# Pair transposes with scores on two row tiles, tables by symmetry and row shifts, and later weights: one change to a linear-attention and Fourier-mix kernel

## The chip, the cores and the metric

One core of one Trainium2 chip. The metric is device time in microseconds of one execution. On one core a run counts as slow when it lies over 1.5% above the fastest of the same kernel.

A ratio below is the mean time of one kernel's fast runs over that of the kernel before's fast runs in the same rounds, with a 95% interval. It is therefore not quite the ratio of the medians that stand beside it.

## The reference

Two parts, one behind the other. The first is an attention with a state that decays per channel, over 4 batches, 8 heads, 768 positions, head width 48:

```python
for t in range(S):
    cur = einsum('bhd,bhe->bhde', u * k_t, v_t)
    y_t = einsum('bhd,bhde->bhe', r_t, state + cur)
    state = w_t[..., None] * state + einsum('bhd,bhe->bhde', k_t, v_t)
```

The second takes y as 768 x 384 per batch:

```python
mixed = real(fft(fft(x, axis=1), axis=2))
u  = x + mixed
un = (u - mean(u)) / sqrt(var(u) + 1e-6)          # over the 384 channels
out = u + relu(un @ w_ch1) @ w_ch2                # 384 -> 1536 -> 384
```

## The kernel before

The attention goes in chunks of 128 positions, 6 a batch, 24 in all. I call them chunk 1 to 24; batch 0 is chunks 1 to 6. For each chunk SyncE loads w, k, r and v (0.2 MB each, in rows of 48 floats), ScalarE takes the logarithm of w, TensorE sums it along the positions, ScalarE takes the exponentials, VectorE and GpSimd scale r and k, TensorE transposes both, and ScalarE copies the transposes to SBUF. The part that the change rewrites, with cuts:

```python
def tr_r(e):                       # r: eight transposes, one for each head
    for h in range(H):
        o0 = 128 * h - 64 * (h % 2)
        ins = e.transpose(psb(trr)[:, 128*h:128*h+128], rflat[:, o0:o0+128], IDB[:, :])
...
op("act", 1000, ... e.activation(rT, psb(trr)[:, :], Copy))      # 1024 columns
...
for hf in range(2):
    def amat(e, hf=hf, ta=ta):     # scores: four matmuls of 256 columns
        for x in range(2):
            q = 2 * hf + x
            ins = e.matmul(ps(ta)[:, 256*x:256*x+256], kT[:, q, :], rT[:, 2*q:2*q+2, :])
```

The Fourier mix is done with matmuls against tables of sines and cosines, which VectorE and ScalarE build at the start. CS and SS serve the sequence axis, DTM and DTP the channel axis. All arguments were computed on VectorE at full width, and DTM had its own argument for each row.

The instructions are put in order by a planner in the kernel itself. It walks through the operations with an assumed duration each and emits every engine's queue in the order of the planned starts. Every queue then runs in that order. For loads it keeps one clock for all queues:

```python
elif o.bytes:
    dma_t = max(dma_t, s + o.dur) + o.bytes / 190.0
    o.end = dma_t + self.DMA_FIX
```

The weights are asked for on GpSimd's queue, because they are converted to bf16 on the way. In the kernel before that was allowed once chunk 3's v had landed.

Of the kernel before, what the change touches and what calls it, by code (L numbers as in the profile page):

```python
# [28 lines left out]
class _Op:  # L29
    __slots__ = ("eng", "fn", "deps", "users", "dur", "key", "tile", "opens", "sem", "inc", "val",  # L30
                 "start", "end", "nd", "idx", "clk", "bytes", "order", "waits", "ready", "last")
# [16 lines left out]
class _Prog:  # L48
# [18 lines left out]
    def op(self, eng, dur, fn, r=(), w=(), key=None, sem=None, nbytes=0):  # L67
# [3 lines left out]
        o.bytes = nbytes  # L71
        for x in r:
            for d in self.wr.get(x, ()):
                o.deps.add(d)
            self.rd.setdefault(x, []).append(o)
            if isinstance(x, _Tile):
                o.tile = (o.tile or []) + [x]
# [18 lines left out]
    def schedule(self):  # L96
# [5 lines left out]
        dma_t = 0.0  # L102
        for o in self.ops:
            for d in o.deps:
                d.users.append(o)
            o.nd = len(o.deps)
            o.ready = 0.0
            if o.nd == 0:
                avail[o.eng].append(o)
        left = len(self.ops)  # L110
        while left:
            best = None
            for e in self.ENGS:
                t = engt[e]
                cand = None
                for o in avail[e]:
                    s = max(t, o.ready)
                    if o.opens:
                        tl = [x for x in o.tile if x.bank is None and x.ops[0] is o][0]
                        if held.get(tl.pool, 0) >= self.caps[tl.pool] or not free_banks:  # L120
                            continue
                        s = max(s, free_banks[0][0])
                    c = (s, o.key, o.idx)
                    if cand is None or c < cand[0]:
                        cand = (c, o)
                if cand and (best is None or cand[0] < best[0]):
                    best = cand
# [4 lines left out]
            if o.opens:  # L132
                tl = [x for x in o.tile if x.bank is None and x.ops[0] is o][0]
                _, tl.bank, prev = heapq.heappop(free_banks)
                held[tl.pool] = held.get(tl.pool, 0) + 1
                o.deps |= set(prev)
            o.start = s
            engt[e] = s + o.dur
            if o.bytes:
                dma_t = max(dma_t, s + o.dur) + o.bytes / 190.0  # L140
# [134 lines left out]
def bass_rwkv6_finch__then__fnet_fourier_mix_kernel(  # L275
# [16 lines left out]
    HF = S // 2 + 1  # L292
    NJ = HID // 128
# [4 lines left out]
    g = _Prog(nc, {"a": 5, "f": 4})  # L298
# [11 lines left out]
    E1 = [sb("e1_%d" % i, [H, D], FP32) for i in range(NB)]  # L310
    E2 = [sb("e2_%d" % i, [H * D + HP], FP32) for i in range(NB)]
    RH = [sb("rh%d" % i, [H, 128], BF16) for i in range(NB)]
    KH = [sb("kh%d" % i, [H, 64], BF16) for i in range(NB)]
    VB = [sb("vb%d" % i, [H, D], BF16) for i in range(4)]
    RTB = [sb("rtb%d" % i, [H, 128], BF16) for i in range(NB)]
# [15 lines left out]
    NMU = [sb("nmu%d" % i, [1], FP32) for i in range(4)]  # L331
# [10 lines left out]
    IDB = sb("idb", [128], BF16)  # L342
# [5 lines left out]
    KI = sb("ki", [HF], FP32)  # L348
    CI = sb("ci", [128], FP32)
    TC = sb("tc", [NC], FP32)  # L350
    TN = sb("tn", [NC], FP32)
    MC = sb("mc", [3], FP32)
    MN = sb("mn", [3], FP32)
    MSH = sb("msh", [3], FP32)
    MB = sb("mb", [3], FP32)
    IS1 = sb("is1", [1], FP32)
    TMPC = sb("tmpc", [4], FP32)
    CP = sb("cp", [1], FP32)
    ALT = sb("alt", [HF], BF16)
# [3 lines left out]
    TF = [sc_u[:, HF * i:HF * i + HF] for i in range(5)] + [sc_h[:, 0:HF]]  # L363
    TG = [sc_h[:, HF * i:HF * i + HF] for i in range(1, 4)]
    TQ = [sc_h[:, HF * 4:HF * 5], sb("tq", [HF], FP32)]
# [7 lines left out]

    def tt(o, a, b, f):
        return lambda e: e.tensor_tensor(out=o, in0=a, in1=b, op=f)  # L375

    def ts(o, a, s1, s2, f0, f1=None):
        if f1 is None:
            return lambda e: e.tensor_scalar(out=o, in0=a, scalar1=s1, scalar2=None, op0=f0)
        return lambda e: e.tensor_scalar(out=o, in0=a, scalar1=s1, scalar2=s2, op0=f0, op1=f1)  # L380

    def stt(o, a, s, b, f0, f1):
        return lambda e: e.scalar_tensor_tensor(out=o, in0=a, scalar=s, in1=b, op0=f0, op1=f1)
# [19 lines left out]
    def small_constants():  # L403
        op("pool", 250, lambda e: e.iota(CI[:, :], [[1, 128]], base=0, channel_multiplier=-1,
                                         allow_small_or_imprecise_dtypes=True), w=["CI"])
        op("pool", 250, lambda e: e.iota(TC[:, :], [[128, NC]], base=0, channel_multiplier=1,
                                         allow_small_or_imprecise_dtypes=True), w=["TC"])
        op("pool", 450, lambda e: e.iota(KI[:, :], [[1, HF]], base=0, channel_multiplier=0,
                                         allow_small_or_imprecise_dtypes=True), w=["KI"])
        op("dve", 210, ts(MSK[:, :], CI[:, :], 0.0, None, ALU.is_gt), r=["CI"], w=["MSK"])  # L410
        op("dve", 210, ts(NLE[:, :], CI[:, :], 0.0, -1.0, ALU.is_ge, ALU.mult), r=["CI"], w=["NLE"])
        op("dve", 270, fill(LB[0][:, :, :], 0.0), w=[("LB", 0)])
        op("dve", 70, fill(ONE[:, :], 1.0), w=["ONE"])
        op("dve", 70, fill(BHPI[:, :], PI / 2), w=["BHPI"])
        op("dve", 490, fill(RH[0][:, :, :], 0.0), w=[("RH", 0)])
        op("dve", 210, ts(IDB[:, :], CI[:, :], 0.0, None, ALU.is_equal), r=["CI"], w=["IDB"])
        op("pool", 580, fill(KH[0][:, :, :], 0.0), w=[("KH", 0)])
        op("dve", 270, fill(LB[1][:, :, :], 0.0), w=[("LB", 1)])
        op("dve", 490, fill(RH[1][:, :, :], 0.0), w=[("RH", 1)])
        op("pool", 580, fill(KH[1][:, :, :], 0.0), w=[("KH", 1)])  # L420
        op("dve", 70, fill(BEPS[:, :], EPS), w=["BEPS"])
        for i in range(2, NB):
            op("dve", 270, fill(LB[i][:, :, :], 0.0), w=[("LB", i)])
            op("dve", 490, fill(RH[i][:, :, :], 0.0), w=[("RH", i)])
            op("pool", 580, fill(KH[i][:, :, :], 0.0), w=[("KH", i)])
        for i in range(2):
            op("pool", 400, fill(XF[i][:, :, 0:64], 0.0), w=[("XFz", i)] + [("XFn", i)])
            op("pool", 400, fill(XF[i][:, :, 446:512], 0.0), w=[("XFz2", i)] + [("XFo", i, c) for c in range(NC)])
            op("pool", 120, fill(X[i][:, :, DM:DM + 4], 0.0), w=[("X", i, c) for c in range(NC)])
# [3 lines left out]
    def tables():  # L433
        sins = []
        op("dve", 100, ts(TN[:, :], TC[:, :], 1.0 / S, None, ALU.mult), r=["TC"], w=["TN"])

        op("dve", 350, ts(TQ[0][:, :], KI[:, :], 0.5, MAGIC, ALU.mult, ALU.add), r=["KI"], w=[("TQ", 0)])
        op("dve", 350, ts(TQ[1][:, :], TQ[0][:, :], MAGIC, -2.0, ALU.subtract, ALU.mult),
           r=[("TQ", 0)], w=[("TQ", 1)])
        op("dve", 550, tt(TQ[0][:, :], KI[:, :], TQ[1][:, :], ALU.add), r=["KI", ("TQ", 1)], w=[("TQ", 0)])  # L440
        op("dve", 550, tt(TQ[1][:, :], TQ[0][:, :], TQ[0][:, :], ALU.mult), r=[("TQ", 0)], w=[("TQ", 1)])
        op("dve", 350, ts(ALT[:, :], TQ[1][:, :], -2.0, 1.0, ALU.mult, ALU.add), r=[("TQ", 1)], w=["ALT"])
        sc = 2.0 * PI / S * (1.0 - 2.0 ** -22)
        for q in range(NC // 2):
            op("dve", 350, ts(TQ[0][:, :], KI[:, :], TN[:, q:q + 1], MAGIC, ALU.mult, ALU.add),
               r=["KI", "TN"], w=[("TQ", 0)])
            op("dve", 350, ts(TQ[1][:, :], TQ[0][:, :], MAGIC, -float(S), ALU.subtract, ALU.mult),
               r=[("TQ", 0)], w=[("TQ", 1)])
            op("dve", 550, stt(TF[q][:, :], KI[:, :], TC[:, q:q + 1], TQ[1][:, :], ALU.mult, ALU.add),
               r=["KI", "TC", ("TQ", 1)], w=[("TF", q)])  # L450
            op("dve", 550, stt(TG[q][:, :], TF[q][:, :], -1.0, TF[q][:, :], ALU.mult, ALU.max),
               r=[("TF", q)], w=[("TG", q)])
            sins.append(act(SS[:, q, :], TF[q][:, :], ACTF.Sin, scale=sc))
            sins.append(act(CS[:, q, :], TG[q][:, :], ACTF.Sin, scale=-sc, bias=BHPI[:, :]))

        p = TC[:, 0:1]
        op("dve", 100, ts(IS1[:, :], p, 62.5, None, ALU.is_gt), r=["TC"], w=["IS1"])
        op("dve", 100, ts(TMPC[:, 0:1], IS1[:, :], -193.0, 129.0, ALU.mult, ALU.add), r=["IS1"], w=["TM0"])
        op("dve", 100, ts(TMPC[:, 1:2], p, 63.0, 193.0, ALU.is_equal, ALU.mult), r=["TC"], w=["TM1"])
        op("dve", 100, tt(TMPC[:, 2:3], TMPC[:, 0:1], TMPC[:, 1:2], ALU.add), r=["TM0", "TM1"], w=["TM2"])  # L460
        op("dve", 100, tt(TMPC[:, 3:4], TMPC[:, 2:3], p, ALU.add), r=["TM2", "TC"], w=["TM3"])
        op("dve", 100, ts(CP[:, :], IS1[:, :], 2.0, -1.0, ALU.mult, ALU.add), r=["IS1"], w=["CP"])
        op("dve", 100, tt(MC[:, 1:2], TMPC[:, 3:4], CP[:, :], ALU.mult), r=["TM3", "CP"], w=["MC1"])
        op("dve", 100, ts(MC[:, 0:1], p, 64.0, None, ALU.add), r=["TC"], w=["MC0"])
        op("dve", 100, ts(MC[:, 2:3], p, -1.0, -1.0, ALU.mult, ALU.add), r=["TC"], w=["MC2"])
        op("dve", 100, fill(MB[:, 0:1], PI / 2), w=["MB0"])
# [323 lines left out]
```

## Time and profile before

| kernel before | us |
|---|---|
| median (lowest to highest of 4 runs) | 237.8 (235.7 to 238.5) |
| span in the profile | 235.8 |
| first hidden-layer matmul (L708) | 72.2 |
| from there to the end | 163.6 |

The first matmul of the first layer (384 to 1536) is a good place to cut the span. Ahead of it the kernel fills its pipeline; behind it TensorE hardly rests.

### The profile page before, as it was taken

The numbers are of one execution on the slowest core, as the hardware profiler recorded it, in microseconds if no ns is written. First come the engines' busy times: TensorE is split into PE (matmuls) and PEld (weight loads), VectorE is DVE, ScalarE is ACT, GpSimd is POOL, SyncE is SP. The second block draws the span as 40 slices with busy tenths as digits, with TensorE's granted clock in tenths as the row PEclk, the third lists the DMA queues.
The fourth block names the chain that finished last, engine by engine and source line by source line (L and its number), as shares of the span: only waits on it lengthen the run. The fifth ranks groups of instructions, "written<-read, shape, count | busy, mean of one in ns | idle before, by whom it ended". The sixth has DMA issues, their size and how long they took to land.

```text
span 235.8 us, 4671 instructions
## 1 busy us (share of the span) xinstructions
PE 200.0 (85%) x1776; PEld 130.1 (55%) x1776; DVE 185.5 (79%) x403; ACT 153.1 (65%) x316; POOL 105.0 (45%) x118
## 2 busy tenths in 40 slices
PE   0765475549769999999998999899989999999994
PEld 0443253436335575666776766467757765666652
DVE  8999999398998389999769998894899866822222
ACT  3554542997466997566887977488969554965340
POOL 7587894629901589282165965401633100000000
PEclk9998555577995999999999999999999999999999
DMA  6999999989970559852365678104200000020102
GB/s 120 211 213 219 183 189 197 214 176 216 198 143 3 100 104 211 191 117 52 81 155 104 133 156 181 38 0 110 60 0 3 36 33 33 3 101 0 70 33 100
DMA packets 105478, 26.45 MB, mean 112 GB/s; under 512 B 100336, under 2 KB 105072, under 8 KB 105456
## 3 DMA queue, kind: packets, MB, share of 16 engines
q1 hardware_dynamic: 103440, 23.80, 47.5%
q0 software_dynamic: 2016, 2.36, 5.9%
q8 instruction: 14, 0.23, 0.4%
q14 instruction: 8, 0.07, 0.1%
HBM read 23.79 MB, written 4.72 MB: 121 GB/s over the span
## 4 chain that ended last, share of the span: by engine, by line
PE 63%; DVE 19%; DMA 9%; ACT 5%; issue 2%; SPq 1%; DVEq 0%; ACTq 0%
PE bank L727 19%; PE bank L708 18%; DMA in_v<-in_v_dram 7%; DVE xf L375 6%; PE bank L648 6%; PE bank L664 5%; PE bank L564 3%; PE bank L583 3%; DVE rh L375 3%; DVE ah L587 3%; DVE x L620 2%; PE bank L684 2%; DMA in_w<-in_w_dram 2%; PE bank L612 2%; PE bank L570 1%
## 5 line engine op out<-in xcount | busy, mean ns | idle before, releaser
L708 PE MATMUL bank<-unt,w 128*128 128x384 bf16 x288 | 58.0, 333 | 0.0
L727 PE MATMUL bank<-w,ht 128*128 128x384 bf16 x288 | 54.1, 326 | 0.0
L717 ACT ACTIVATE ht<-bank 128x384 bf16<-128x384 f32 x80 | 37.9, 500 | 19.2 <-PE bank L708 19.0
L587 DVE TENSOR_TENSOR ah<-bank,msk 128x512 bf16<-128x512 f32 x48 | 31.1, 679 | 8.2 <-PE bank L583 8.1
L375 POOL TENSOR_TENSOR vtd<-in_v,dc 128x384 f32<-128x384 f32 x24 | 21.1, 884 | 35.8 <-DVE dc L545 32.7
L708 PEld LDWEIGHTS bank<-unt,w 128*128 128x128 bf16 x288 | 26.9, 99 | 16.1 <-issue 1.0
L727 PEld LDWEIGHTS bank<-w,ht 128*128 128x128 bf16 x288 | 26.9, 98 | 15.3
L573 ACT ACTIVATE rtb<-bank 128x1024 bf16<-128x1024 bf16 x24 | 24.6, 1025 | 15.0 <-PE bank L564 14.8
L732 DVE SCALAR_TENSOR_TENSOR osb<-bank,rstd,uf 128x384 f32<-128x384 f32 x24 | 14.8, 615 | 17.2 <-PE bank L727 16.7
L375 DVE TENSOR_TENSOR xf<-x 128x192 bf16<-128x192 f32 (+1 forms) x48 | 26.6, 593 | 0.1
L375 POOL TENSOR_TENSOR rk<-rk,ub 128x384 f32<-128x384 f32 x24 | 25.2, 1051 | 1.3
L375 POOL TENSOR_TENSOR rk<-in_r,in_k 128x384 f32<-128x384 f32 x24 | 25.4, 1060 | 0.0
L564 PE MATMUL bank<-idb,rh 128*128 128x128 bf16 x192 | 17.2, 242 | 8.7 <-DVE rh L375 8.1
L375 POOL TENSOR_TENSOR kh<-in_k,e_0 128x384 bf16<-128x384 f32 x8 | 8.8, 1096 | 31.3 <-ACT e_0 L538 31.3
L575 ACT ACTIVATE ktb<-bank 128x512 bf16<-128x512 bf16 x24 | 14.3, 597 | 9.5 <-PE bank L570 9.3
L564 PEld LDWEIGHTS bank<-idb,rh 128*128 128x128 bf16 x192 | 13.7, 108 | 11.8 <-DVE rh L375 8.5
L612 PE MATMUL bank<-vb,ah 128*128 128x48 bf16 x192 | 15.8, 189 | 5.0 <-DVE ah L587 4.9
L583 PE MATMUL bank<-rtb,ktb 128*128 128x256 bf16 x96 | 17.4, 309 | 1.8 <-ACT rtb L573 1.1
L525 PE MATMUL bank<-lb,msk 128*128 128x384 bf16 x24 | 9.4, 391 | 11.1 <-ACT lb L389 11.1
L713 DVE TENSOR_SCALAR ht<-bank 128x384 bf16<-128x384 f32 x16 | 8.8, 552 | 12.6 <-PE bank L708 12.6
L612 PEld LDWEIGHTS bank<-vb,ah 128*128 128x128 bf16 x192 | 13.1, 100 | 9.5 <-DVE ah L587 6.5
L389 ACT ACTIVATE lb<-in_w 128x384 bf16<-128x384 f32 x24 | 12.5, 523 | 5.9 <-DMA in_w<-in_w_dram 5.9
(111 smaller groups left out, 403.1 us busy)
## 6 DMA issues: line engine op xcount, KB each, us to landing
in_w<-in_w_dram SPq DMA_DIRECT2D x24, 192.0 KB, 3.7
in_k<-in_k_dram SPq DMA_DIRECT2D x24, 192.0 KB, 3.7
in_r<-in_r_dram SPq DMA_DIRECT2D x24, 192.0 KB, 3.7
in_v<-in_v_dram SPq DMA_DIRECT2D x24, 192.0 KB, 3.5
out_dram<-osb SPq DMA_DIRECT2D x24, 192.0 KB, 1.9
w<-in_moe_w_ch_dram POOLq DMA_DIRECT2D x6, 384.0 KB, 9.7
ub<-in_u_dram SPq DMA_DIRECT2D x1, 192.0 KB, 3.8
```

What stands on the lines that cost most here:

```text
L375: return lambda e: e.tensor_tensor(out=o, in0=a, in1=b, op=f)
L564: ins = e.transpose(psb(trr)[:, 128 * h:128 * h + 128], rflat[:, o0:o0 + 128], IDB[:, :])
L573: op("act", 1000, lambda e: e.activation(rT[:, :, :].rearrange("p h t -> p (h t)"), psb(trr)[:, :], ACTF.Copy), r=[trr], w=[("RTB", i2)])
L575: op("act", 570, lambda e: e.activation(kT[:, :, :].rearrange("p h t -> p (h t)"), psb(trk)[:, 0:512], ACTF.Copy), r=[trk], w=[("KTB", i2)])
L583: ins = e.matmul(ps(ta)[:, 256 * x:256 * x + 256], kT[:, q, :], rT[:, 2 * q:2 * q + 2, :].rearrange("p h t -> p (h t)"))
L587: op("dve", 660, lambda e, hf=hf, ta=ta: e.tensor_tensor(out=ah[:, 4 * hf:4 * hf + 4, :], in0=ps(ta)[:, :].rearrange("p (h t) -> p h t", t ...
L612: ins = e.matmul(ps(ty)[:, D * h:D * h + D], ah[:, h, :], vb[:, h, :], start=True, stop=first)
L648: return e.matmul(ps(t)[:, 0:HF], xf[:, s, off:off + 128], tab[:, s, :], start=a, stop=z)
L708: ins = e.matmul(ps(t)[:, 0:384], W1[:, m, 128 * j:128 * j + 128], unt[:, m, :], start=(m == 0), stop=(m == NM - 1))
L717: op("act", 475, lambda e, j=j, t=t, ht=ht: e.activation(ht[:, j, :], ps(t)[:, 0:384], ACTF.Relu), r=[t], w=[("HT", q % 2, j)])
L727: ins = e.matmul(ps(t)[:, 0:DM], ht[:, j, 128 * x:128 * x + 128], W2[:, j, :], start=(j == 0), stop=(j == NJ - 1))
L732: op("dve", 540, lambda e, kb=kb, t=t, o=o: e.scalar_tensor_tensor(out=o[:, :], in0=ps(t)[:, 0:DM], scalar=rstd[:, kb:kb + 1], in1=uf[:, k ...
```

## The change

Its intent is to take work from TensorE in every chunk and from VectorE at the start. In its core, with cuts marked:

```diff
 def tr_r(e):
-    for h in range(H):
-        o0 = 128 * h - 64 * (h % 2)
-        ins = e.transpose(psb(trr)[:, 128*h:128*h+128], rflat[:, o0:o0+128], IDB[:, :])
+    for h in range(HP):                                  # four, one for a pair of heads
+        ins = e.transpose(psb(trr)[:, 128*h:128*h+128], rflat[:, 128*h:128*h+128], IDB[:, :])
...
-    ins = e.matmul(ps(ta)[:, 256*x:256*x+256], kT[:, q, :], rT[:, 2*q:2*q+2, :])
+    for q in range(HP):                                  # eight of 128 columns, two row tiles
+        for x in range(2):
+            ins = e.matmul(ps(ta[x])[:, 128*q:128*q+128], kT[64*x:64*x+D, q, :],
+                           rT[64*x:64*x+D, q, :])
...
-op("act", 470, act_ps(e1, tce), r=[tce], w=[("E1", i2)])         # exponential to SBUF
+op("act", 470, ... activation(ps(tce), ps(tce), Exp), w=[tce])   # it stays in PSUM
...
-op("dve", 350, tt(xf[:, c, 256:447], ...
+op("dve" if b == 0 else "pool", ..., tt(xf[:, c, 256:447], ...
...
-           r=[("in", "v", 2)], w=[("W1", q)], ...        # weights after chunk 3's v
+           r=[("in", "v", 5 % NIN)], w=[("W1", q)], ...  # weights after chunk 6's v
...
+op("act", 1290, ... preload_act_table_set("trig_and_small"), w=["TRIG"])   # first on ScalarE
+# arguments for a quarter period; the mirror and the sign flips fill the rest
+# DTM and DTP: matmuls of CS and SS with shifted identities, two evictions each
+# 24 pairs of warm-up matmuls with planned times from 8 us on
```

The planner's keys and durations are new too, so all queues are in another order, and its DMA clock is 200 in place of 190. It also plans GpSimd's operations and most of VectorE's on one shared clock (`port_t`), so that in the plan none of them overlap.

## The prediction

> **What bounds the kernel now.** I read the page first (busy shares, then the span in forty slices), then the chain of work that ended last, then busy time per engine in three stretches cut at the first matmul of the hidden layer (line L708), then the instruction groups and single timelines.
>
> ```profile
> PE 200.0 (85%) x1776; PEld 130.1 (55%) x1776; DVE 185.5 (79%) x403; ACT 153.1 (65%) x316; POOL 105.0 (45%) x118
> ...
> PE   0765475549769999999998999899989999999994
> ...
> DVE  8999999398998389999769998894899866822222
> ...
> PEclk9998555577995999999999999999999999999999
> ```
>
> One digit is 5.9 us. The kernel has two halves: in the first twelve or so slices VectorE stands at 8 and 9 while TensorE is half idle and on a half clock; after that TensorE is full to the end. The stretches say the same in microseconds:
>
> ```profile
> core 0: us, PE busy (x) PEld busy (x) DVE busy (x) ACT busy (x) POOL busy (x), PEclk, DMA share, GB/s
> 0.00:72.40 72.40, 43.41 (x363) 27.88 (x364) 66.80 (x149) 42.17 (x79) 47.93 (x60) 0.77 0.99 186
> 72.40:94.00 21.60, 20.89 (x198) 13.01 (x196) 16.03 (x30) 17.90 (x41) 14.68 (x16) 0.90 0.55 111
> 94.00:235.80 141.80, 135.70 (x1219) 89.24 (x1217) 102.69 (x226) 93.06 (x198) 42.41 (x43) 1.00 0.31 75
> ```
>
> So the time is the start (72.4 us, VectorE busy for 66.8 of it, with DMA near full) plus what TensorE still has to do then (busy 156.6 of 163.4 us). A saving on VectorE counts before 72.4, a saving on TensorE after it. The chain of waits agrees, and shows a hole:
>
> ```profile
> 24.82 16.01 DMA in_v<-in_v_dram
> ...
> 72.45 0.96 PE bank L708 x3
> ...
> 226.82 5.86 PE bank L727 x36
> 232.78 0.62 DVE osb L732
> ```
>
> A load that usually lands in 3.5 us takes 16, because the six weight transfers were issued from 22.6 us on among the first batch's inputs. The groups that the change touches:
>
> ```profile
> L573 ACT ACTIVATE rtb<-bank 128x1024 bf16<-128x1024 bf16 x24 | 24.6, 1025 | 15.0 <-PE bank L564 14.8
> L583 PE MATMUL bank<-rtb,ktb 128*128 128x256 bf16 x96 | 17.4, 309 | 1.8 <-ACT rtb L573 1.1 <-ACT ktb L575 0.6
> L564 PE MATMUL bank<-idb,rh 128*128 128x128 bf16 x192 | 17.2, 242 | 8.7 <-DVE rh L375 8.1 <-ACT vb L389 0.5
> L620 DVE TENSOR_TENSOR x<-bank,vtd 128x384 f32<-128x384 f32 x24 | 13.2, 550 | 3.7 <-PE bank L615 2.1 <-PE bank L612 1.4
> L375 DVE TENSOR_TENSOR rh<-in_r,e_0 128x384 bf16<-128x384 f32 x8 | 6.4, 802 | 0.0
> ```
>
> A matmul's mean is a latency, not a rate. Rates come from a timeline of a full-clock stretch: start to start 163 ns for 384 columns, 55 ns for a 128-column transpose, 108 ns for 256 columns, 25 ns for the 48-column ones.
>
> **What the Trainium skill says.** (1) "SBUF — State Buffer", section "Who interferes with whom": a VectorE instruction with two SBUF inputs and a GpSimd instruction that reads SBUF lock each other out. The trace agrees: the rh product (two SBUF inputs) means 1.10 us over its eight in the first 72.4 us, the x sum of the same width with one PSUM input 0.55. (2) "TensorE: Matmul & The Clock Gate", Part 1: an idle TensorE drops to half clock. Agrees: granted clock 0.50 between 24 and 41 us, where eight transposes take 1.03 us against 0.61 at full clock. (3) "TensorEngine Tiling (Array Packing)", "Key Properties": row tiles run in parallel, but changing the tiling mode drains the engine. The kernel before has one mode only, so its trace cannot show either. (4) "ScalarE: Activation LUTs", "What ACT_TABLE_LOAD costs": about 1283 ns a load; the trace has three of 1283.
>
> **The change part by part.**
>
> *Scores.* r is transposed in head pairs, 4 transposes for 8 (saves 4 x 55 = 0.22 us of TensorE a chunk); its eviction is 128x512 for 128x1024 (about 0.60, as ktb's 597 ns, for 1.03 on ScalarE); four 256-column score matmuls (0.43 us) become eight of 128 columns on two row tiles. If pairs overlap that is 0.22 us, if not 0.44, and a drain on each side may add up to one 0.18 us latency. The output matmuls go from 16 to 12: 16 x 25 = 0.41 to 4 x 42 + 8 x 25 = 0.37. TensorE a chunk before: 3 x 0.163 + 0.10 + 0.44 + 0.22 + 0.43 + 0.17 + 0.41 = 2.26 us. After: between 1.79 (overlap, no drain) and 2.3; I take 1.95.
>
> *VectorE up to the first hidden-layer matmul.* Before, by group in 0 to 72.4 us: tables 24.3, their small columns 1.8, masks 1.6, fills 2.6, attention and mix 47.0; sum 77.3 us of instruction spans, which overlap to 66.8 us busy (factor 0.86). After, counted in the new order up to the third mean and variance: table steps 12, half as wide, about 0.41 each (estimate from 0.48 to 0.88 at full width) = 5.0; two mirrors 1.6; small ones and negated identity 1.1; masks 1.9; fills 22 x 0.1 = 2.2; ah 16 x 0.66 = 10.5; xf 8.0; dc 4.3; rh now reads PSUM, 8 x 0.55 = 4.4 (was 8.8); x 7 x 0.55 = 3.9; state in two halves 14 x 0.32 = 4.5; three blocks of uf, statistics 3.8; the hcr copies (1.7) go to GpSimd and the sign flips go away. Sum 51.2, times 0.86 = 44 us. The idle time of VectorE there was 5.6 us; the later start of chunk 0 (three table halves and a second table load on ScalarE come before its first Ln, which now is ready at about 8.5 us and not at 5.4) adds perhaps 2, and from the third variance to the first hidden matmul it is about 1.5 us. Together 53.
>
> *DMA in the start.* Weights are now asked for only when the sixth chunk has landed. Before chunk 9's scores, which stand just ahead of the first hidden matmul in TensorE's new order, 9 x 0.79 + 0.2 MB of inputs and 2.36 MB of weights must land: 9.6 MB at 0.195 MB/us is 49 us, plus 2 for the first, plus 4 for Ln, sums, Exp, product, transposes, eviction: 55. So both limits meet; first hidden matmul at **55 us** instead of 72.4.
>
> *TensorE after that.* Before, still to do at 72.4: 576 x 0.163 = 93.9 (two layers), 72 x 0.163 = 11.7 (sequence DFT), 54 x 0.163 = 8.8 (channel DFT), 3.5 (transposes of un), 16.3 chunks x 2.26 = 36.8; sum 154.7, taken in 160.2 us, a factor of 1.036. After: the same but 15.3 x 1.95 = 29.8; sum 147.7, times 1.036 = 153.0.
>
> *The rest.* 24 pairs of 384-column warm-up matmuls all stand before the first hidden matmul (24 x 2 x 0.163 = 7.8 us, where TensorE has 30 us to spare); they should lift the clock of 0.77 there. The row-shift matmuls cost some 1.1 us and six ScalarE evictions 2.9 us in the same place. xf's odd half goes to GpSimd for 18 chunks (18 x 0.66 = 11.8 us off VectorE), which is later and mostly hidden.
>
> Sum: 55 + 153.0 + 3.1 (last matmul to end, as before) = 211.1 us of span; the time stands 2.2 above the span in the profiled run: **213 us**, 10.6% less.
>
> **The rivals.**
> 1. *The weights become the wait.* They are issued late, on GpSimd's queue behind five vtd products; GpSimd has 4.1 us of work a chunk (1.06 + 1.05 + 0.88 + 1.11). For it: vtd waited 32.7 us for dc before. Against: the first layer's three transfers need only land by 53. If it holds, the first hidden matmul slips to about 63 and the time is 221.
> 2. *Row tiles give nothing*: drains of 2 x 0.18 us and no overlap put a chunk at 2.3. TensorE's remainder is then 153.1 x 1.036 = 158.6, the time 219.
> 3. *Other engines become the bound later.* GpSimd takes xf and hcr, so more locks with VectorE, and a chunk's sums must now wait for an earlier chunk's masks. VectorE's load from 94 us on was 72%, and falls, which speaks against; a stall factor of 1.07 would give 218.
> 4. *The start is faster still*, as VectorE has less lockout and TensorE a full clock: first hidden matmul at 49, stall factor 1.02, time 205.
>
> **Range and chances.** Rivals 1 to 3 each cost 5 to 8 us and hardly come all together; rival 4 gives 8. So 204 to 222. To stay within 2% (233.6) the whole gain of the start would have to vanish: faster 0.96, same 0.03, slower 0.01.
>
> **What would show it.** The first hidden-layer matmul near 55 us (before 60 or the start is mis-sized); no 16 us load in the first batch; granted clock above 0.9 from 15 us on; VectorE's busy time near 44 us before that matmul; rh at 0.55 us; eviction rtb at 0.60; score matmuls of a chunk within 0.25 to 0.45 us in the timeline; after the first hidden matmul TensorE busy 95% or more. The prediction is wrong if TensorE after that point falls under 90%, or if that first matmul waits on a weight transfer.

## The result, and the profile after

| | before | after |
|---|---|---|
| median, us | 237.8 | 221.0 |
| runs | 4 (235.7 to 238.5) | 4 (220.3 to 223.9; the one at 223.9 is slow) |
| ratio of the fast runs | | 0.930 (0.923 to 0.936) |

The result is correct, 7% faster, and within the predicted range near its upper end. The profile that came with it fell in the slow state (span 222.0 us). I ran the same kernel once more among the experiments (c0_after below) and read that profile, which is of a fast run.

The page of the changed kernel, busy shares and the span in slices of 5.5 us:

```profile
PE 193.3 (87%) x1758; PEld 120.5 (54%) x1758; DVE 150.2 (68%) x348; ACT 145.6 (66%) x322; POOL 112.0 (51%) x140
...
PE   1397855757788989999999999999999999999994
...
DVE  8769955503488986698988888599857654634322
...
PEclk9999995579696999999999999999999999999999
```

VectorE has lost 35 us of work and is no longer full at the start. A hole stands in the ninth to eleventh slices (44 to 61 us): VectorE at 0 to 4, TensorE at 5 to 7, its clock at 6 to 9 after 5 in the two slices ahead. The same kernel in stretches, with the columns as in the prediction, cut at its first hidden matmul (L729, 71.2 us):

```profile
0.00:71.20 71.20, 47.37 (x447) 27.91 (x447) 46.04 (x127) 43.80 (x92) 42.06 (x56) 0.86 1.02 191
71.20:93.00 21.80, 20.93 (x194) 13.04 (x191) 17.20 (x35) 17.17 (x40) 18.39 (x22) 1.00 0.71 147
93.00:221.00 128.00, 124.97 (x1123) 79.56 (x1121) 86.95 (x188) 84.60 (x191) 51.58 (x64) 1.00 0.31 76
```

Set beside the lines of before: VectorE's busy time in the start fell from 66.8 to 46.0 us, yet the first hidden matmul moved only from 72.2 to 71.2. Nearly the whole gain lies behind it: 163.6 us before, 221.1 - 71.2 = 149.9 us after. The four engines have 24 to 29 us to spare each in the start; only DMA is full (share 1.02).

The groups of the change came out as planned (line, engine, operation, output and input, count, busy us, mean ns):

```profile
L393 POOL TENSOR_TENSOR xf<-x 128x191 bf16<-128x191 f32 x18 | 11.4, 631 | 24.1 <-DVE x L647 23.2
...
L573 DVE TENSOR_TENSOR rh<-bank,in_r 128x384 bf16<-128x384 f32 x24 | 13.2, 550 | 6.9 <-ACT bank L549 6.7
...
L593 ACT ACTIVATE rtb<-bank 128x512 bf16<-128x512 bf16 x24 | 14.2, 594 | 3.7 <-PE bank L584 3.7
```

Why the start did not get shorter is to be seen in the hole. Busy times there:

```profile
39.00:51.00 12.00, 8.74 (x63) 5.14 (x64) 4.54 (x13) 6.37 (x16) 3.34 (x4) 0.67 1.22 197
51.00:60.00 9.00, 6.43 (x39) 3.69 (x38) 2.69 (x7) 3.32 (x7) 7.13 (x10) 0.84 1.11 215
```

VectorE works 7 of these 21 us, ScalarE 10, and DMA is over its mean share. ScalarE's timeline shows what it waits for (start, duration, what, and in brackets the idle time ahead of it with what ended it):

```profile
45.90 0.52 ACT L407 ACTIVATE vb<-in_v 128x384 bf16<-128x384 f32 x1 [4.77 <-DMA in_v<-in_v_dram]
46.33 0.58 ACT L593 ACTIVATE rtb<-bank 128x512 bf16<-128x512 bf16 x1
46.81 0.51 ACT L407 ACTIVATE lb<-in_w 128x384 bf16<-128x384 f32 x1
47.22 0.48 ACT L512 ACTIVATE dtm<-bank 128x384 bf16<-128x384 f32 x1
...
54.37 0.52 ACT L407 ACTIVATE vb<-in_v 128x384 bf16<-128x384 f32 x1 [2.56 <-DMA in_v<-in_v_dram]
55.59 0.52 ACT L407 ACTIVATE lb<-in_w 128x384 bf16<-128x384 f32 x1 [0.70 <-DMA in_w<-in_w_dram]
```

A queue runs in order. The first two lines with a long wait are the copy of chunk 8's v and, just behind, the logarithm of chunk 10's w; the last two are chunk 9's v and chunk 11's w. All four belong to batch 1. Between and behind them stand what batch 0 needs for its first hidden matmul: the evictions of the tables DTM and DTP (L512, L513), and at 56.02 us the third and last eviction of its Fourier matmul. So batch 0, whose own inputs have long landed, waits for loads of batch 1; and behind that last eviction come most of its channel matmuls and all its statistics, normalisation and transposes, 15.2 us up to the first hidden matmul at 71.2. The chain of waits names the two loads:

```profile
36.56 9.32 DMA in_v<-in_v_dram
45.90 0.52 ACT vb L407
...
51.61 3.96 DMA in_w<-in_w_dram
55.59 0.52 ACT lb L407
```

A load of 0.2 MB takes 9.3 us here and 3.7 to 4.0 in the median. What makes it slow are the weights: GpSimd asks for W1 and part of W2 from 28 to 36 us and for the rest at 43.5 us. The page's part on DMA queues gives their cost (packets, MB, share of the 16 engines' span; q0 carries the weights alone):

```profile
q1 hardware_dynamic: 103440, 23.80, 50.5%
q0 software_dynamic: 2016, 2.36, 6.5%
```

6.5% of 221.1 us is 14.4 us of all 16 engines for the weights. That is more than the 2.36 MB written suggest: 6.1 us a MB against 0.505 x 221.1 / 23.8 = 4.7 us a MB for the rest, loads and stores together. (The weights are read as twice as many bytes, in f32.) While they travel they take most of what the engines give. First 9 to 28 us, ahead of the weights, then 36 to 44 us:

```profile
q1 hardware_dynamic: 19543, 3.70, 99.2%
```

```profile
q0 software_dynamic: 805, 1.15, 81.0%
q1 hardware_dynamic: 2249, 0.42, 34.4%
```

The loads fall from 3.70 / 19 = 0.195 MB/us to 0.42 / 8 = 0.05. One more thing stands in the chain: between 49.6 and 63 us it holds ten warm-up matmuls (L791), 2.4 us together.

### The profile page after: what moved, and what is told of

The parts are those of the page before. It is cut to its first block, busy times and chain, and to the rows that moved or that the text cites. A ratio compares the mean times of both kernels' runs of the same rounds, so it can differ in the third digit from the quotient of the medians.

```text
span 222.0 us, 4609 instructions
## 1 busy us (share of the span) xinstructions
PE 192.7 (87%) x1758; PEld 120.2 (54%) x1758; DVE 150.0 (68%) x348; ACT 145.6 (66%) x322; POOL 111.9 (50%) x140
## 3 DMA queue, kind: packets, MB, share of 16 engines
q0 software_dynamic: 2016, 2.36, 6.4%
## 4 chain that ended last, share of the span: by engine, by line
PE 74%; DMA 12%; DVE 6%; POOL 3%; issue 2%; SPq 1%; ACT 1%; DVEq 0%
PE bank L748 21%; PE bank L729 20%; DMA in_w<-in_w_dram 8%; PE bank L672 7%; PE bank L688 5%; DMA in_v<-in_v_dram 4%; PE bank L603 3%; PE bank L590 2%; PE bank L791 2%; PE bank L584 2%; PE bank L547 2%; PE bank L641 2%; PE bank L705 2%; PE bank L543 2%; PE bank L638 2%
## 5 line engine op out<-in xcount | busy, mean ns | idle before, releaser
L729 PE MATMUL bank<-unt,w 128*128 128x384 bf16 x288 | 57.3, 334 | 0.0
L729 PEld LDWEIGHTS bank<-unt,w 128*128 128x128 bf16 x288 | 26.7, 99 | 16.8 <-issue 1.1
L647 DVE TENSOR_TENSOR x<-bank,vtd 128x384 f32<-128x384 f32 x24 | 13.3, 554 | 18.5 <-PE bank L641 18.3
L393 POOL TENSOR_TENSOR xf<-x 128x191 bf16<-128x191 f32 x18 | 11.4, 631 | 23.1 <-DVE x L647 19.9
L547 PE MATMUL bank<-lb,nle 128*128 128x384 bf16 x24 | 8.8, 368 | 12.9 <-ACT lb L407 12.4
L407 ACT ACTIVATE vb<-in_v 128x384 bf16<-128x384 f32 x24 | 12.5, 521 | 9.8 <-DMA in_v<-in_v_dram 7.3
L690 DVE TENSOR_TENSOR uf<-bank,x 128x384 f32<-128x384 f32 x24 | 13.0, 548 | 8.5 <-PE bank L688 8.4
L710 ACT ACTIVATE unt<-bank 128x384 bf16<-128x384 f32 x24 | 11.8, 490 | 9.7 <-PE bank L705 9.6
L407 ACT ACTIVATE un<-uf,agg 128x384 bf16<-128x384 f32 x24 | 14.6, 610 | 4.8 <-DVE agg L696 4.8
L791 PE MATMUL bank<-idw,msk 128*128 128x384 bf16 x48 | 13.9, 383 | 4.0 <-DVE idw L397 4.0
L593 ACT ACTIVATE rtb<-bank 128x512 bf16<-128x512 bf16 x24 | 14.3, 594 | 3.7 <-PE bank L584 3.7
L573 DVE TENSOR_TENSOR rh<-bank,in_r 128x384 bf16<-128x384 f32 x24 | 13.2, 550 | 4.8 <-ACT bank L549 4.6
```

The source lines that it names most:

```text
L393: return shared(lambda e: e.tensor_tensor(out=o, in0=a, in1=b, op=f))
L407: return lambda e: e.activation(o, a, f, **kw)
L593: op("act", 570, lambda e: e.activation(rT[:, :, :].rearrange("p h t -> p (h t)"), psb(trr)[:, 0:512], ACTF.Copy), r=[trr], w=[("RTB", i2)])
L647: op("dve", 530, lambda e: e.tensor_tensor(out=xb[:, c, 0:DM], in0=ps(ty)[:, 0:DM], in1=vtd[:, :, :].rearrange("t h d -> t (h d)"), op=ALU ...
L729: ins = e.matmul(ps(t)[:, 0:384], W1[:, m, 128 * j:128 * j + 128], unt[:, m, :], start=(m == 0), stop=(m == NM - 1))
L791: ins = e.matmul(ps(tw)[:, 0:384], MSK[:, :], IDW[:, :])
```

## The experiments

Twelve kernels ran, all correct, in four calls. The kernel before had a median of 237.5, 239.1, 237.5 and 236.7 us in these. All are edits of the changed kernel except b2_wlate. "Ln 11" is the start of chunk 11's logarithm on ScalarE, which stands just ahead of batch 0's last Fourier eviction (a dash where the order or the kernel is another). "First" is the first hidden-layer matmul in the profile and "rest" is the profile's span less that. Where the profiled run is slow, the table says so. Medians are over all runs, slow ones too.

| run | call | median us | ratio to before | Ln 11 | first | rest |
|---|---|---|---|---|---|---|
| c0_after | 1 | 222.3 | 0.937 (0.932 to 0.942) | 55.6 | 71.2 | 149.9 |
| e1_move | 1 | 223.5 | 0.944 (0.938 to 0.950) | - | 69.3 | 149.7 |
| e1b_move | 1 | 226.0 | 0.953 (0.947 to 0.958) | - | 73.3 | 149.9 |
| e2_w2late | 1 | 216.9 | 0.915 (0.910 to 0.920) | 49.1 | 65.1 | 151.4 |
| e11_wlate | 2 | 215.8 | 0.894 (0.886 to 0.902) | 51.1 | 66.7 (slow) | 150.4 |
| e3_tiles | 2 | 223.0 | 0.926 (0.920 to 0.933) | 56.9 | 71.9 (slow) | 151.6 |
| e4_tr8 | 2 | 225.8 | 0.945 (0.938 to 0.952) | 55.6 | 69.2 | 153.5 |
| e7_nowarm | 2 | 224.7 | 0.928 (0.919 to 0.938) | 57.4 | 74.5 (slow) | 149.9 |
| e12_wdep | 3 | 213.3 | 0.900 (0.896 to 0.904) | 41.9 | 61.0 | 150.5 |
| b2_wlate | 3 | 235.1 | 0.984 (0.978 to 0.990) | - | 70.3 | 163.5 |
| e5_rh_sbuf | 3 | 224.3 | 0.946 (0.941 to 0.950) | 55.2 | 71.2 | 151.4 |
| e13_back | 4 | 222.5 | 0.941 (0.937 to 0.944) | 55.5 | 71.0 | 152.1 |

The theories were two. A: the order of the queues of TensorE and ScalarE holds batch 0 back, as the work of batch 1 stands in front. B: the DMA engines hold everything back, as 2.36 MB of weights travel among the inputs that this order needs. A rival to both was that VectorE still sets the start.

**c0_after** is the changed kernel unchanged, for its profile and for the noise.

> The changed kernel once more, unedited, for a profile in the fast state and as the reference of this batch: about 220.5 us (4 fast runs so far lay between 220.3 and 221.3), span about 219, first hidden-layer matmul near 69 us.

Its runs are all fast, at 221.2 to 222.9 us; they and the first hidden matmul (71.2) lie some 2 us above what was expected. The ratio (0.937) and that of the first result (0.930) have overlapping intervals; differences under 1% between calls are therefore not read.

**e1_move** takes the sums of chunk 10 and their logarithm from in front of batch 0's Fourier mix and puts them behind it, by hand after the planner has run:

```diff
+    for e in ("act", "pe"):
+        q = g.order[e]
+        a = max((anchor[e, 0, j] for j in range(3)), key=q.index)   # last Fourier matmul, eviction
+        for le, o in late:                                          # chunk 10: Ln and its sums
+            if le == e and q.index(o) < q.index(a):
+                q.remove(o)
+                q.insert(q.index(a) + 1, o)
+                a = o
```

> Only the Ln of chunk 9 on ScalarE and its two sums on TensorE are moved in the queues, to behind batch 0's sequence DFT and its evictions. Theory A (the start is long because both queues stand in order at chunk 9, whose load shares DMA with the weights): ScalarE's wait of 4.3 us on that load leaves the start, the first hidden-layer matmul comes 4 to 5 us earlier and nearly all of it reaches the end: 216 us. Theory B (volume of DMA sets the start, whatever the order): first hidden-layer matmul and time as before the edit, within 1 us: 220.5.

(This expectation and the next two count the chunks from 0: their chunk 9 is chunk 10 here, their chunk 7 chunk 8.) The first hidden matmul came at 69.3 us and the time did not fall: the median is 223.5 us, and the two fast runs mean 221.8 for 222.2 in c0_after. (The ratio in the table leaves the profiled run, the fastest, out.) TensorE now waited 3.8 us for a table's eviction and 6.3 us in two waits for logarithms.

**e1b_move** also moves chunk 8's copy of v, which still stood in front on ScalarE:

```diff
+        if n == 7:
+            late.append(("act", o_vb))
```

> As the run before, and chunk 7's copy of v on ScalarE (which waited 6.3 us for its load, ahead of the table evictions) is moved behind batch 0's DFT too. Theory A: both ScalarE waits (4.3 and 6.3 us) leave the start; first hidden-layer matmul at about 60 us, time about 211. Theory B: no change, 220.5. If only the first hidden matmul moves and the end does not, the later part has another bound than TensorE.

Now batch 0's mix starts at 44.8 us, and TensorE stands just behind it, at the moved sums. Its timeline:

```profile
44.80 0.34 PE L683 MATMUL bank<-cs,xf 128*128 128x385 bf16 x1 [0.91 <-DVE xf L393]
...
56.75 0.50 PE L550 MATMUL bank<-lb,nle 128*128 128x384 bf16 x1 [9.13 <-ACT lb L407]
```

The wait was moved, not removed: first hidden matmul at 73.3 us, and the time 1.7% above c0_after. Theory A falls as far as these two moves go. Moving the sums of chunks 10 to 12 behind the first hidden matmul altogether was not measured: the order of the PSUM banks then locked up, and the kernel did not build.

**e2_w2late** leaves all orders alone and only asks for W2 later, behind batch 0's last reversed copy on GpSimd:

```diff
+    q = g.order["pool"]
+    for o in w2_ops:
+        q.remove(o)
+    a = max(q.index(o) for o in hcr_ops[:3])
+    q[a + 1:a + 1] = w2_ops
```

> Only the three transfers of the second weight matrix (half of the weight bytes, 1.18 MB) are moved later in GpSimd's queue, behind batch 0's mirrored copies, about 20 us later; no other queue changes. Theory A and B both say that chunk 9's load lands about 6 us earlier (1.18 MB at 0.2 MB/us). A: TensorE's stand of 8.7 us shrinks to 3, first hidden matmul near 64, time 215. B: inputs needed before the first hidden matmul still set it, 2 to 6 us earlier, time 215 to 219. If neither moves, the weights are not what delays chunk 9.

First hidden matmul at 65.1 us, 6 us earlier, and the median 5.5 us lower. Theory B stands. (Whoever moves weights should know a tie in this kernel: their request reads the buffer of chunk 6's v, which chunk 11's v takes over, so that load must wait for all six transfers. Here SyncE's request for it ends at 65.05 us, when the last of W2 lands. In c0_after the weights have landed at 52 us and it is asked for at 63.9.)

**e11_wlate** asks for both later, W1 just ahead of batch 0's first reversed copy and W2 behind chunk 8's k product:

```diff
+    a = min(q.index(o) for o in hcr_ops[:3])
+    q[a:a] = w1_ops
+    a = q.index(kh_ops[7]) + 1
+    q[a:a] = w2_ops
```

> The changed kernel with the weights' transfers asked later still: the three of W1 just before batch 0's first Fourier copy on GpSimd, the three of W2 behind chunk 8's k product; the queues of the other engines are the same instruction for instruction. Theory B (until the first hidden-layer matmul the DMA engines are the limit, and every byte of weights that lands before the last needed input delays it): the first hidden matmul comes at about 60 us, against 65.1 with only W2 moved and 71.2 with none moved; median 211 to 214 us. Theory A (the order of TensorE's queue alone sets that time): no change from the changed kernel, 221 to 223. A third outcome, W1 now landing too late and becoming the wait itself: first hidden matmul waiting on a W1 transfer, 217 to 222.

Its two fast runs took 213.2 and 213.9 us, as theory B said. The other two, the profiled one among them, took 217.7 and 218.9. In that slow profile GpSimd, having nothing else to do, asked for W1 at 39.4 us already, and chunk 11's w, asked for right behind it, took 11 us. (The two fast runs were not profiled; that W1 was asked for later in them is not seen.) The chain of waits:

```profile
40.11 10.96 DMA in_w<-in_w_dram
51.08 0.52 ACT lb L407
```

**e12_wdep** removes that chance. W1 must wait until chunk 12's w has landed:

```diff
+    for o in w1_ops:
+        o.deps.add(ld["w", 11])
```

> As e11_wlate, and W1's three transfers are in addition held until chunk 12's w input has landed, so that they cannot overtake an input that the sums ahead of the first hidden-layer matmul need. If those inputs, delayed by the weights, set the start: the 11 us that chunk 12's w took in e11_wlate shrink to about 4, the first hidden matmul comes at 57 to 61 us, and the median is 207 to 212, in few or no slow executions. If W1 then lands too late and is the wait itself: first hidden matmul at 62 to 66 and 213 to 217. If the order of the queues alone sets the start: 221.

(The 11 us load was chunk 11's w; the expectation names chunk 12's, which is asked for together with it.) Both now land ahead of the weights, chunk 12's in 3.85 us, as expected. The chain of waits:

```profile
38.62 3.85 DMA in_w<-in_w_dram
42.77 1.82 POOL w L521 x3
44.58 0.95 POOL hcr L683 x2
```

First hidden matmul at 61.0 us, at the end of what was expected; all six runs are fast, 212.5 to 214.7 us, some 1 us above the expected range. This is the best median of all versions and beats both kernels: 0.900 of before. (The two fast runs of e11_wlate are as fast.) What holds the start now:

```profile
0.00:61.00 61.00, 42.30 (x448) 24.91 (x449) 46.71 (x127) 44.02 (x92) 42.28 (x57) 0.96 1.03 196
```

DMA is as full as ever; what counts is which bytes come first. In the order of SyncE's queue 40 loads of 0.197 MB are asked for up to chunk 11's w, 7.9 MB. Alone they take 7.9 / 0.195 = 40 us, and chunk 11's logarithm starts at 41.9. With 2.36 MB of weights among them it is 10.2 MB and 52 us, and in c0_after it starts at 55.6. The 13.7 us between the two buy 10.2 of the time to the first hidden matmul. No group of TensorE waits for a weight. In the chain GpSimd has taken a place (the request for W1 and the copies behind it), and from 42.8 us on it hardly stops.

**b2_wlate** does the same to the kernel before, to see what held its start: W1 moves to 40.5 us on GpSimd's queue and W2 to 55.3 (43 and 59 were expected).

```diff
+    a1, a2 = q[39], q[49]        # in GpSimd's order
+    for o in w1 + w2:
+        q.remove(o)
+    a = q.index(a1)
+    q[a:a] = w1
+    a = q.index(a2)
+    q[a:a] = w2
```

> The kernel before, with its weights asked for later on GpSimd's queue (W1 at about 43 us, W2 at about 59 us, in place of 22 to 28 us); no other queue changes. If the kernel before was held by VectorE until its first hidden-layer matmul (72.4 us), as the prediction reads it: that matmul stays within 2 us and the time within 1% of before. If the kernel before was in truth held by the DMA engines too: the matmul comes 4 us or more earlier and the time is 2% lower.

The matmul moved from 72.2 to 70.3 us, within the 2 us of the first expectation, and the time by 1.6%, between the two. VectorE stays full in the stretch before it:

```profile
0.00:70.30 70.30, 42.70 (x363) 27.32 (x364) 68.59 (x149) 41.95 (x79) 48.35 (x60) 0.91 1.01 189
```

68.6 of 70.3 us. This fits the prediction's reading that VectorE held the start of the kernel before, though no run takes work from VectorE alone there. The weights cost it some 2 us, where they cost the changed kernel 10 (one profile each).

**e5_rh_sbuf** tests the rival, VectorE. The exponential goes to SBUF again, which makes the r product dearer; all queues keep their order:

```diff
-        op("act", 470, ... activation(ps(tce), ps(tce), Exp), w=[tce])
+        op("act", 470, ... activation(E1[i2], ps(tce), Exp), w=[tce, ("E1", i2)])
-           in0=ps(tce)[:, 0:DM], in1=rt[:, :, :]
+           in0=rt[:, :, :], in1=E1[i2][:, :, :]
```

> The changed kernel with the exponential of a chunk's sums written to SBUF again, as before, so that the r product on VectorE has two SBUF inputs (1.10 us each in the start of the kernel before, 0.55 with the PSUM input); the order of every queue is kept. If VectorE still sets the first hidden matmul: some ten products at +0.5 us, the start 4 to 5 us later, median 225 to 227. If the DMA engines set it: first hidden matmul within 2 us of 71, median 220.5 to 223.5.

VectorE's busy time in the start rose by 5.1 us, and the first hidden matmul stayed at 71.2:

```profile
0.00:71.20 71.20, 47.16 (x447) 27.20 (x447) 51.18 (x127) 43.96 (x92) 43.62 (x57) 0.87 1.04 194
```

Five microseconds more on VectorE do not move it: VectorE does not set the start of the changed kernel. The median is 224.3, 0.8 us above what was expected; in the profile the rest has grown, 151.4 for 149.9 us.

**e7_nowarm** cuts the warm-up matmuls to one column:

```diff
-                ins = e.matmul(ps(tw)[:, 0:384], MSK[:, :], IDW[:, :])
+                ins = e.matmul(ps(tw)[:, 0:1], MSK[:, :], IDW[:, 0:1])
```

> The warm-up matmuls cut to one column, their number and order kept. They cost 13.9 us of TensorE, most of it before 42 us where it waits for data. If what they buy is clock (granted share 0.67 to 0.84 in 39 to 60 us, full later): the clock in 60 to 90 us falls and the median rises by 1 to 4 us. If the start is bound by DMA and the throttle answers to load: the first hidden matmul stays at 70 to 72 us and the median within 1 us, or falls by up to 2 us where warm-ups stand in front of ready work.

Two of four runs are slow and the interval is wide: nothing is shown about the time beyond 1%. The clock did answer. In the hole it fell to the half, against 0.74 in c0_after (first line e7_nowarm, second c0_after):

```profile
39.00:60.00 21.00, 10.08 (x58) 5.58 (x59) 4.63 (x13) 6.20 (x15) 6.58 (x9) 0.50 1.11 196
```

```profile
39.00:60.00 21.00, 15.17 (x100) 8.83 (x101) 7.24 (x19) 9.69 (x22) 10.48 (x14) 0.74 1.17 205
```

From 60 to 90 us it is 0.93 in the one and 0.94 in the other. What the warm-ups are worth in time this run does not show. Its fast runs mean 221.8 us, for 221.3 in e3_tiles of the same call.

The last three runs ask about the rest, which fell by 13.7 us where 7.2 were predicted.

**e3_tiles** runs the four even heads first and then the four odd ones, so that neighbours use the same row tile:

```diff
-            for q in range(HP):
-                for x in range(2):
+            for x in range(2):
+                for q in range(HP):
```

> Only the order of the eight score matmuls of a chunk differs: the four of the even heads, then the four of the odd heads, so that no neighbours lie on different row tiles. If the gain of the score matmuls comes from neighbours on two row tiles running at the same time, it is lost: the group goes from 0.33 us at full clock to 0.43 or more, 15 times 0.1, and the median rises by about 1.7 us. If it comes only from the shorter operands and from the missing change of tiling, nothing changes: within 0.5 us of the changed kernel.

The time did not change. Its fast runs mean 221.3 us, and the group of eight takes 0.34 us from its start to the next group's start, where c0_after has 0.33. But this does not mean that the tiles take turns. TensorE's timeline merges neighbours; asked with ever narrower windows it gives the single starts, as each line begins at the first matmul that the window still holds. In c0_after:

```profile
129.34 0.65 PE L729 MATMUL bank<-unt,w 128*128 128x384 bf16 x3
129.93 0.40 PE L603 MATMUL bank<-rtb,ktb 48*128 48x128 bf16 x8
129.93 0.40 PE L603 MATMUL bank<-rtb,ktb 48*128 48x128 bf16 x7
130.00 0.33 PE L603 MATMUL bank<-rtb,ktb 48*128 48x128 bf16 x6
130.00 0.33 PE L603 MATMUL bank<-rtb,ktb 48*128 48x128 bf16 x5
130.11 0.22 PE L603 MATMUL bank<-rtb,ktb 48*128 48x128 bf16 x2
130.26 0.34 PE L543 MATMUL bank<-lb,msk 128*128 128x384 bf16 x1
```

The eight start in pairs, the two of a pair within 4 ns, the pairs 0.05 to 0.07 us apart. One 128-column transpose takes 0.055 us, so two matmuls are at work at once. The trace does not name a matmul's row tile; that a pair lies on two tiles is inferred. In e3_tiles they start in pairs too, 14 ns apart:

```profile
126.56 0.41 PE L603 MATMUL bank<-rtb,ktb 48*128 48x128 bf16 x8
126.58 0.39 PE L603 MATMUL bank<-rtb,ktb 48*128 48x128 bf16 x7
126.63 0.34 PE L603 MATMUL bank<-rtb,ktb 48*128 48x128 bf16 x6
126.64 0.33 PE L603 MATMUL bank<-rtb,ktb 48*128 48x128 bf16 x5
```

So the other order did not take the overlap away, and this run cannot price it. What takes its gain back stands at the edges of the group. L729's three start 0.163 us apart from 129.34, so that a fourth would start at 129.83; the scores start at 129.93. Behind the last pair (130.11) the next group starts 0.15 us later and not 0.055. These are two pauses of 0.10 us, one at each change of tiling. The kernel before has none:

```profile
133.25 0.65 PE L708 MATMUL bank<-unt,w 128*128 128x384 bf16 x3
133.74 0.60 PE L583 MATMUL bank<-rtb,ktb 128*128 128x256 bf16 x4
134.18 0.65 PE L708 MATMUL bank<-unt,w 128*128 128x384 bf16 x3
```

With the pause ahead of them a chunk's scores cost TensorE 0.43 us, against 0.44 before (medians of ten and eleven groups behind 95 us). Row tiles bought the scores next to nothing here: the overlap saves some 0.2 us, and the two pauses cost as much. Point 3 of what the prediction takes from the Trainium skill, tiles in parallel and a drain at a change of tiling, fits both; no run isolates either.

**e4_tr8** puts the eight r transposes and the eviction of 1024 columns back, with the scores left on two row tiles (the second four transposes are copies that nothing reads):

```diff
-            for h in range(HP):
-                ins = e.transpose(psb(trr)[:, 128*h:128*h+128], rflat[:, 128*h:128*h+128], IDB[:, :])
+            for h in range(2 * HP):
+                x = h % HP
+                ins = e.transpose(psb(trr)[:, 128*h:128*h+128], rflat[:, 128*x:128*x+128], IDB[:, :])
-        ... psb(trr)[:, 0:512], Copy)
+        ... psb(trr)[:, 0:1024], Copy)
```

> The r transposes go back to eight of one head each, and their eviction back to 1024 columns, with the order of TensorE's and ScalarE's queues kept; the score matmuls stay on two row tiles. If the pair transposes carry a part of the gain after the first hidden matmul: 15 times 0.22 us on TensorE is +3.3 us, and up to +4.5 if the wider evictions on ScalarE (about 0.45 us more each) also hold the chain up. If TensorE's work after the first hidden matmul is not what sets the end: within 1 us.

The rest grew from 149.9 to 153.5 us, and the fast runs mean 225.5 us, 4.2 above e3_tiles of the same call. The eviction is dear again, and TensorE stays full:

```profile
L594 ACT ACTIVATE rtb<-bank 128x1024 bf16<-128x1024 bf16 x24 | 24.5, 1021 | 5.5 <-PE bank L585 5.5
```

```profile
69.20:222.70 153.50, 149.31 (x1373) 96.05 (x1371) 104.06 (x222) 107.74 (x231) 70.17 (x85) 1.00 0.37 86
```

149.31 busy, 3.4 more than in c0_after (145.9): the 15 chunks at 0.22 us that the prediction counted. The transposes and their eviction, not the scores, are what a chunk gained.

**e13_back** gives back to VectorE what batches 1 to 3 moved to GpSimd (18 odd halves of the fold, 9 reversed copies), to see whether relief of VectorE took TensorE's waits away:

```diff
+    for o in sorted(back, key=lambda o: o.start):
+        g.order["pool"].remove(o)
+        o.eng = "dve"
+        q = g.order["dve"]
+        q.insert(next(i for i, x in enumerate(q + [None]) if x is None or x.start > o.start), o)
```

> The changed kernel with the work that it moved from VectorE to GpSimd for batches 1 to 3 put back on VectorE (18 odd halves of the fold, 9 reversed copies), at the places of VectorE's queue that follow from the planned start times; the queues of TensorE and ScalarE are the same. Open is why the stretch after the first hidden-layer matmul lost more than its TensorE work: 163.4 to 149.9 us. If relief of VectorE took away the waits of TensorE there (3.3 us in that stretch before, 0.6 after): the waits come back, the stretch rises by 2 to 3 us, median 224 to 226. If they went for another reason (fewer chunks left in the stretch, clock): the stretch within 1 us of 149.9 and the median within 1 us of the changed kernel's, 221 to 223.

The profile's rest rose by 2.2 us, but the profiled run is the slowest of the seven (224.9); the median did not rise (222.5 for 222.3 in another call; ratios 0.941 and 0.937, overlapping). TensorE's waits behind the cut are three:

```profile
PE bank L548 <- DVE st L630: 0.7, 1, 0.7
PE bank L642 <- DVE ah L609: 0.4, 1, 0.4
PE bank L604 <- DVE ht L739: 0.3, 1, 0.3
```

1.4 us together, for 0.6 in c0_after and 3.3 in the kernel before. This run does not decide: relief of VectorE accounts for a part of those waits at most.

## Why the prediction was right or wrong

The total fell in the range because two of its terms were off in opposite directions. Predicted were 55 us to the first hidden matmul and 156.1 us from there to the end of the span; the fast profile has 71.2 and 149.9.

*The step that failed* is the one on DMA in the start, which counts what must land "before chunk 9's scores, which stand just ahead of the first hidden matmul in TensorE's new order". It put the last load at 51 and 4 us of work behind it. The profile has the last load that holds batch 0 at 55.6 and 15.6 us behind it.

1. *What stands behind the load, 11.6 us of the miss.* The prediction named TensorE's order only, took the last attention work ahead of the matmul as what waits, and let batch 0's mix run beside the loads. In ScalarE's order chunk 11's logarithm stands ahead of batch 0's last Fourier eviction, so nearly the whole of the mix behind the Fourier matmul comes after that load.
2. *When the load lands, 4.6 us of the miss.* 10.2 MB and not 9.6 come first. And the weights were taken as bytes that simply add up, while it can be chosen whether they come first. They share the DMA engines with inputs asked for before them. The Trainium skill says so in "DMA: Bandwidth & Descriptors", section "Queues, rings and completion order": each DMA engine takes turns between the queues that have work for it, packet by packet. The traces agree: loads at 0.05 MB/us beside the weights and 0.195 without them, the 9.3 us load of the changed kernel and the 11 us load right behind W1 in e11_wlate, against 3.85 us once W1 waited. Between c0_after and e12_wdep only the moments of the six weight requests differ, and 10.2 us of the start go.

The planner had made the same mistake as the prediction: its single DMA clock lets the weights queue behind the inputs, so in its plan they delay no load that was asked for before them. That this is why it chose the order is argued from the code, not tested.

*VectorE up to the first hidden matmul* was right in itself: 46.0 us against the 44 worked out, the r product at 550 ns. It was a true saving on an engine that thereby left the critical path, and e5_rh_sbuf shows that 5 us of it could be given back without moving the first hidden matmul. Of the 20.8 us saved, 1.0 showed there.

*The remainder* was mis-sized the other way. Of the working, the chunk is near: with 0.43 us for the scores in place of the 0.38 implied, 2.00 us for 1.95. The transposes are worth what was said (e4_tr8: 3.6 us of the rest). The term that was off is the factor 1.036 from the kernel before, kept for the kernel after. With the scores as measured the sum is 147.7 + 15.3 x 0.05 = 148.5 us, and the stretch without its last 3.1 us took 146.8: a factor of 0.99, worth 7 us. (Below one, as the sum takes every chunk as a full one. In the kernel before the state is updated in 20 of 24 chunks, L600 x80, and decays in 16, L597 x16; by the prediction's own terms that is some 0.1 us a chunk too much, an estimate, in both sums.) Before, TensorE was busy for 156.6 us of 163.4; after, for 145.9 of 149.9. Its waits for other engines behind the cut fell from 3.3 to 0.6 us, and its clock in the first 22 us behind it was 0.90 before and 1.00 after, worth up to 2.2 us by estimate. The two come to at most 4.9 of the 7 us, and why they went is not settled: e13_back shows a part of the waits at most, and none of the runs isolates the clock.

*The eviction, the scores, TensorE's share* (594 ns, 0.33 us in the timeline without the pause ahead, 97%) came as the prediction's list said. *The clock* did not: it expected over 0.9 from 15 us on, and the hole has 0.67 and 0.84.

*The rivals.* Rival 1 gave the right time, 221, with a mechanism that is half right. The weights were the trouble, but no group of TensorE waited on one; the loads of inputs were held up by them. e11_wlate and e12_wdep show it: asking for them later, which rival 1 feared, made the start faster. Rival 2, row tiles that give nothing, was right in the outcome for the scores and wrong in the mechanism: the overlap is there, and two pauses of 0.10 us take it back, not two of 0.18 without overlap. Its price of 2.3 us a chunk did not come (2.00). Rival 3 did not come. Rival 4's factor of 1.02 was close for the rest, its start was not.

## What to carry to other kernels

When a start is near two limits, relief of one shows nothing until the other is moved. Before trusting a saving, list, on every in-order queue and not only on the busiest, what stands ahead of the point you time, and add up the bytes that it needs. A large transfer on another queue did not wait its turn behind loads already asked for (0.05 MB/us left to them here): hold it with a dependency on the last load that must go first, and place it by the moment it is needed, not by the moment its engine is free. And before saying that two things do not overlap, look at single starts: the total of a group can hide an overlap and a pause of the same size.

## What the Trainium skill lacked or had wrong

- "TensorEngine Tiling (Array Packing)" says that a change of the tiling mode drains the engine; no page that I found gives a time for it. Here 0.10 us was lost at each change, ahead of and behind eight 48-row score matmuls. The eight started in pairs within 4 ns, so that the overlap and the two pauses cancelled (0.43 us a chunk for 0.44).
- "DMA: Bandwidth & Descriptors" has trn2 rates by the size of a transfer and a least transfer for line rate, but no trn2 rate for rows shorter than that. Loads of 0.2 MB in rows of 192 bytes, many at a time, ran at 196 GB/s here with the engines full (9 to 28 us).
- The same page has no price for a transfer that converts f32 to bf16: 6.1 us of the 16 engines a MB written, against 5.1 a MB for the plain loads (99.2% of 19 us for 3.70 MB).
- No page that I found says that a load's issue on SyncE itself grows long while such transfers are under way: between 28 and 52 us of c0_after six issues took 2.0 to 4.0 us and one in e11_wlate 7.9, though the work that had to free their buffers was done 13 us or more ahead. From 5 to 28 us they took 0.7 to 1.8. The trace does not say what they waited for.
